# Fewer blocks turned through DRAM, and a turned load moved down its queue, in a forward-and-backward adaLN block on one core

## The chip, the core and the metric

The kernel runs on one core of a Trainium2 chip, written in Bass and Tile. The core has a matrix engine (TensorE, in the profile PE for matmuls and PEld for weight loads), a vector engine (VectorE, DVE), a scalar engine (ScalarE, ACT), GpSimd (POOL) and SyncE (SP). In this kernel SP issues nearly all loads and POOL nearly all stores: each of the two issues its DMAs strictly in the order of its program, and a DMA that has to wait for data or for a free buffer holds back all that stand behind it on that engine. The metric is the device time of one execution, in microseconds, as the median of three timed runs; one further execution is profiled.

## The reference: what is computed

One block of a network with a spectral mixer and a channel MLP, both modulated by a conditioning vector, and its gradient. S = 2048 tokens, D = 1024 channels, F = 3584 hidden units, all in bf16:

```python
def _A_ref(x, w_r, w_i):                       # spectral mixer
    X = rfft2(x.astype(float32)) * (w_r + 1j * w_i)
    return irfft2(X, s=(S, D)).astype(bfloat16)
def _B_ref(x, w1, b1, w2, b2):                 # channel MLP
    return gelu(layernorm(x) @ w1 + b1) @ w2 + b2
mod = silu(c) @ w_mod                          # six rows: sa, ca, ga, sb, cb, gb
h = layernorm(x) * (1 + ca) + sa
x = x + ga * _A_ref(h, w_r, w_i)
h = layernorm(x) * (1 + cb) + sb
x = x + gb * _B_ref(h, w1, b1, w2, b2)
```

The kernel returns the forward output and the gradients for grad_out of x, w_r, w_i, w1, b1, w2, b2, c and w_mod.

## The kernel before

Tokens are worked on in four blocks of 512, hidden units in 28 pieces of 128 (`fc`), channels in eight chunks of 128. Matmuls contract over the 128 partitions, so each matrix is needed with its contracted axis on the partitions. Where DRAM holds it the other way round, a transposing DMA (DMA_TRANSPOSE in the profile, `dma_start_transpose` in the code) turns it on the way in. The profile cuts the digits off the names: `d_n` is `d_n3`, `d_gx` is `d_gx1`, `d_x` is `d_x1`.

The stages follow each other on TensorE:

1. **Modulation, and the ph product beside the forward mixer.** ph is the gradient that reaches the hidden layer: w2 times the incoming gradient, which has been multiplied by gb (`gBoT`). `ph_part` (L803) computes for one `fc` and the four token blocks 32 matmuls into `pp`, and stores the result to `d_ph`. Its weights come from `wt`, a ring of two slots. Each slot holds a turned tile of 256 hidden units of w2, two `fc`; `load_w2t` (L339) loads tile `fg` on SP into slot `fg % 2`. Fourteen tiles pass through the ring. For the last four `fc` only two of the four token blocks are computed here and the other two a little later. Beside these products VectorE and ScalarE finish the mixer: `consume_fwd` (L849) adds, normalises and modulates one token block after the other and stores the normalised rows to `d_n3` on SP (L863).
2. **The MLP forward.** `z_block` (L916) loads a token block of `d_n3` turned (`n3Ta` for the first block, `n3Tb` for the next, L919), multiplies with w1 (`pz`, L931), applies the gelu and its derivative, and stores the hidden activations `d_hh` and their gradients `d_gz` by POOL. The seven w1 tiles are loaded by `load_w1` (L877) beside the last tiles of w2: two, one, and four of them.
3. **Back through w1.** For each token block `b`, `pg_pass` (L1088) multiplies gz with w1 turned, and VectorE and ScalarE go back through the two layer norms, with the block's rows `n3u`, `n2u` and `got` loaded on SP. The result is stored to `d_gx1` by POOL (L1312). In the same loop `turn` (L1250) prepares later stages: it loads a piece of `d_hh` or `d_gz` turned into one of two buffers `hb` (SP, L1253) and stores it in its new orientation to `d_hhT` or `d_gzT` (POOL, L1255). Ten `fc` of hh (10 to 19) are turned in the blocks b = 1 and 2, four pieces of gz in the block b = 3. At the end of the loop the last of the four `gB` tiles (the incoming gradient times gb) is computed by VectorE; two are loaded from `d_gB` (L1321).
4. **gw2 products and the backward mixer.** The gradient of w2: for each `fc`, `gw2_product` runs two groups of 16 matmuls of a turned hh block with the four `gB` tiles (L1221). The first two `fc` have their hh in `fbuf`; the others are loaded by `hh_load` within `pieces` (L1397) some products ahead: plainly from `d_hhT` for `fc` 10 to 19, and as a transposing DMA from `d_hh` for the others (tiles `hht`, `hhsA`, `otl`). Between the products stand the matmuls of the backward mixer.
5. **gw1 products.** The gradient of w1, in seven groups of 512 hidden units (L1440). Each group needs two tiles `gzh` of 1 MB, which `gw1_load` fetches: for the first group plainly from `d_gzT`, for the others by a transposing DMA from `d_gz`.

The order on each engine is written out by the program, with a scheduler that places instructions by priority; `tc.issue_after(x)` and `behind(y, x)` keep an instruction behind another one in the order. TensorE, VectorE and ScalarE have the same instructions in the same order in both kernels; only the queues of SP and POOL differ.

Of the kernel before, what the change touches and what calls it, by code (L numbers as in the profile page):

```python
# [11 lines left out]
BF16 = mybir.dt.bfloat16  # L12
# [5 lines left out]
P = 128  # L18
# [3 lines left out]
NT = S // P  # L22
# [9 lines left out]
BW = S // NB  # L32
# [3 lines left out]
def kernel(  # L36
# [24 lines left out]
    nc = tc.nc  # L61
# [5 lines left out]
    dram = ctx.enter_context(tc.tile_pool(name="dram", bufs=1, space=bass.MemoryType.DRAM))  # L67
# [40 lines left out]
    d_n3 = dram.tile([S, D], BF16, name="d_n3")  # L108
# [6 lines left out]
    d_SF = dram.tile([P, 4, 4, 512], BF16, name="d_SF")  # L115
    d_SI = dram.tile([P, 2, 4, 256], BF16, name="d_SI")
    d_E = dram.tile([P, 2, 8, 256], BF16, name="d_E")
    d_hhT = dram.tile([10, P, NT * P], BF16, name="d_hhT")
    d_gzT = dram.tile([4, P, NT * P], BF16, name="d_gzT")
    d_gmod = dram.tile([6 * D], BF16, name="d_gmod")  # L120
    d_ph_v = d_ph.rearrange("(fc p) s -> p fc s", p=P)
    d_hh_v = d_hh.rearrange("(fc p) s -> p fc s", p=P)
# [212 lines left out]
    go_f = tok_flat(grad_out)  # L335

    w2t_in = [None]

    def load_w2t(fg):  # L339
        w2t_in[0] = nc.sync.dma_start_transpose(out=wt[:, fg % 2], in_=B_w2[fg * 256:(fg + 1) * 256, :])  # L340

    x4s = [reg.tile([P, 4, D], BF16, name=f"x4_{i}", tag=f"uv{i}") for i in range(4)]
    fbuf = reg.tile([P, 4, 4, D], BF16, name="fbuf", tag="fr")
# [171 lines left out]
    def behind(ins, later):  # L515
        tc.add_manual_dep(ins.ins, later.ins.name, mybir.DependencyInfo(mybir.DependencyClass.NoSync, mybir.DependencyReason.DATA),
                          reason="order")
# [348 lines left out]
                  act_copy, act_copy, act_copy, consume_fwd, "fr")  # L866

    n3_sqrt, n3_norm = sqrt_in[0], norm_in[0]
    w1s = []
    w1_v = B_w1.rearrange("(c p) f -> p c f", p=P)  # L870

    def load_w1(n):
        for _ in range(n):
            g = len(w1s)
            wtile = reg.tile([P, NDC, BW], BF16, name=f"w1_{g}", tag=W1T[g])
            with tc.issue_after(w2t_in[0].ins):
                nc.sync.dma_start(out=wtile[:], in_=w1_v[:, :, g * BW:(g + 1) * BW])  # L877
            w1s.append(wtile)

    PH_KEEP = NFC - 4  # L880
# [35 lines left out]
    def z_block(b, g0, g1):  # L916
        n3T = n3Ts[b % 2]
        if g0 == 0:
            nc.sync.dma_start_transpose(out=n3T[:], in_=d_n3[b * BW:(b + 1) * BW, :])  # L919
        for g in range(g0, g1):  # L920
            n = b * 7 + g
            zb, av, bv, sg, ph = gts[n % 2]
# [3 lines left out]
            for k in range(4):  # L926
                fc = g * 4 + k
# [28 lines left out]
            for k in range(4 if b >= 2 else 0):  # L956
                fc = g * 4 + k
# [103 lines left out]
    def load_gz(b, g):  # L1061
        n = b * 7 + g
        gzs[b, g] = gzr[n % 8 // 2][:, n % 2]
        gz_in[0] = nc.sync.dma_start(out=gzs[b, g], in_=d_gz_v[:, g * 4:(g + 1) * 4, b * BW:(b + 1) * BW])
# [4 lines left out]
    for g in range(7):  # L1069
        wtile = reg.tile([P, 4, D], BF16, name=f"w1T_{g}", tag=W1T[g])  # L1070
        for k in range(4):
            fc = g * 4 + k
# [127 lines left out]
    def hh_in_frame(fc):  # L1200
        hh_in[0] = nc.sync.dma_start_transpose(out=hh_f[:, fc], in_=d_hh[fc * P:(fc + 1) * P, :])
# [9 lines left out]
    def sums3_ga(b, p4):  # L1211
        halves_sum(acc3[1], p4, b == 0, b == 3)
# [37 lines left out]
    def turn(dst, src, mm):  # L1250
        hb = reg.tile([P, mm, NT * P // mm], BF16, name="hb", tag=("gm", "sb")[turned[0] % 2])
        turned[0] += 1
        nc.sync.dma_start_transpose(out=hb[:], in_=src)  # L1253
        with tc.issue_after(gx_in[0].ins) if gx_in[0] else ExitStack():
            nc.gpsimd.dma_start(out=dst, in_=hb[:].rearrange("p a b -> p (a b)"))  # L1255

    for b in range(NB):
# [9 lines left out]
        if b > 0:  # L1267
            for g in range(7):
                load_gz(b, g)
            with tc.issue_after(gz_in[0].ins):  # L1270
                for k in range(5 if b < 3 else 0):
                    fc = 5 + 5 * b + k
                    turn(d_hhT[fc - 10], d_hh[fc * P:(fc + 1) * P, :], NT)
                for k in range(0 if b < 3 else 4):
                    turn(d_gzT[k], d_gz[0:512, k * 512:(k + 1) * 512], 4)
            if b == 2:
                hh_in_frame(0)
                hh_in_frame(1)
            for h in range(2):
                for _ in pg_pass(b, h, lambda k: ps_f):  # L1280
                    pass
            with tc.issue_after(last_pg[0].ins):
                sums3_ga(b - 1, au)
                if b == 2:
                    gb1_rows()
# [94 lines left out]
    w1g = {}  # L1380

    def gw1_load(fg):
        for k in range(2):
            if fg == 0:
                ins = nc.sync.dma_start(out=w1g["gz"][k][:].rearrange("p (j a) b -> p j (a b)", j=2),
                                        in_=d_gzT[2 * k:2 * k + 2].rearrange("j p n -> p j n"))
                continue
            ins = nc.sync.dma_start_transpose(out=w1g["gz"][2 * (fg % 2) + k][:],
                                              in_=d_gz[fg * 512:(fg + 1) * 512, k * 1024:(k + 1) * 1024])
        return ins  # L1390
# [5 lines left out]

    def pieces():  # L1397
        def hh_load(fc):
            if 10 <= fc < 20:
                hh_in[0] = nc.sync.dma_start(out=hh_s[hh_o[fc]].rearrange("p a b -> p (a b)"), in_=d_hhT[fc - 10])  # L1400
            else:
                hh_in[0] = nc.sync.dma_start_transpose(out=hh_s[hh_o[fc]], in_=d_hh[fc * P:(fc + 1) * P, :])
# [143 lines left out]
```

## Time and profile before

| | |
|---|---|
| timed runs | 1427.33, 1438.67 and 1431.37 us, median 1431.37 |
| profiled execution | 1444.82 us |
| its span | 1443.0 us, mean granted TensorE clock 0.985 |
| DVE, ACT, POOL busy | 1071.9, 744.5, 371.4 us |
| SP's DMA queue (q1) | 319558 packets, 207.18 MB, 55.5% of the 16 DMA engines' span |
| POOL's DMA queue (q0) | 37920 packets, 128.00 MB, 25.4% |

The span is what the profiler recorded between the first and the last instruction; the profiled execution's own time has some two microseconds around it, and lies 13.45 us above the median. The granted clock is the share of its full speed at which TensorE ran. The page cuts the span into 40 slices and gives the busy share of each engine in tenths:

```profile
PE   5999999799999999999999999969999999999998
DMA  9963647979787776697999499994889987767994
```

TensorE is at 9 nearly everywhere; besides the first slice two slices stand out, a 7 (the eighth slice, about 253 to 289 us) and a 6 (the 27th, about 938 to 974 us).

### The profile page before, as it was taken

To read this page: it belongs to the slowest core of one execution; us is meant where nothing else is said; L and a number is where in the kernel's file an instruction comes from. 1 tells how busy PE (TensorE), PEld (TensorE's weight loads), DVE (VectorE), ACT (ScalarE), POOL (GpSimd) and SP (SyncE) were. 2 spreads that over 40 slices of the span, in tenths; PEclk is the share of its full clock that TensorE was granted. 3 is DMA by queue.
4 is the path that set the end of the run, shared out by engine and by line. 5 is a ranking of instruction groups with operands and counts; after the bars stand their busy time and mean duration, and the time that the engine had idled before them with its cause. 6 is when DMAs were issued, how large, how long until landed. Compare 5 with 4: busy or idle time off the path is not lost. (4 is left out here: it accounts for less than half of the span.)

```text
span 1443.0 us, 18578 instructions
## 1 busy us (share of the span) xinstructions
PE 1370.7 (95%) x6839; PEld 662.9 (46%) x6963; DVE 1071.9 (74%) x1503; ACT 744.5 (52%) x1063; POOL 371.4 (26%) x482
## 2 busy tenths in 40 slices
PE   5999999799999999999999999969999999999998
PEld 2445674344444444444444444324554555444443
DVE  5898889867698877886610898949678668998633
ACT  4775766547977765666306564314433435444211
POOL 5601622200212122212110011011356541322323
PEclk8999999989999999999999999989999999999999
DMA  9963647979787776697999499994889987767994
GB/s 333 298 215 103 170 131 242 238 211 342 244 249 261 232 246 235 202 277 234 292 283 228 117 302 300 226 268 145 228 258 289 267 203 223 209 168 190 279 240 147
DMA packets 357569, 336.37 MB, mean 233 GB/s; under 512 B 207690, under 2 KB 297312, under 8 KB 357350
## 3 DMA queue, kind: packets, MB, share of 16 engines
q1 hardware_dynamic: 319558, 207.18, 55.5%
q0 software_dynamic: 37920, 128.00, 25.4%
q8 instruction: 54, 0.88, 0.3%
q14 instruction: 37, 0.30, 0.1%
HBM read 168.35 MB, written 117.49 MB: 198 GB/s over the span
## 5 line engine op out<-in xcount | busy, mean ns | idle before, releaser
L806 PE MATMUL pp<-gBoT,wt 128*128 128x512 bf16 x874 | 197.2, 383 | 13.6 <-DMA wt<-in_B_w_dram 12.5
L1088 PE MATMUL pg<-w1T,gzr 128*128 128x512 bf16 x877 | 195.0, 379 | 3.7 <-ACT gn3b L1103 1.7
L1440 PE MATMUL gw1acc<-gzh,n3n 128*128 128x512 bf16 x877 | 194.1, 379 | 1.0
L806 PEld LDWEIGHTS <-wt 128*128 128x128 bf16 x896 | 87.9, 98 | 117.5 <-DMA wt<-in_B_w_dram 13.0
L1088 PEld LDWEIGHTS <-gzr 128*128 128x128 bf16 x896 | 86.5, 98 | 110.7 <-issue 8.2
L931 PEld LDWEIGHTS <-w 128*128 128x128 bf16 x896 | 87.2, 98 | 107.3 <-issue 2.7
L1440 PEld LDWEIGHTS <-n3n 128*128 128x128 bf16 x896 | 87.3, 98 | 105.1 <-issue 1.3
L931 PE MATMUL pz<-n3Ta,w 128*128 128x512 bf16 x439 | 98.2, 379 | 1.8 <-ACT gt L934 1.3
L931 PE MATMUL pz<-n3Tb,w 128*128 128x512 bf16 x436 | 98.0, 379 | 0.7 <-issue 0.2
L934 ACT ACTIVATE gt<-pz,b_col 128x512 bf16<-128x512 f32 x112 | 73.3, 683 | 37.4 <-PE pz L931 36.9
L988 PEld LDWEIGHTS <-hhA 128*128 128x128 bf16 x608 | 58.9, 98 | 71.9 <-issue 1.6
L1221 PE MATMUL gw2acc<-gB,hhsA 128*128 128x512 bf16 x406 | 91.2, 379 | 0.5
L1444 ACT CAST gwo<-gw1acc 128x512 bf16<-128x512 f32 x49 | 28.5, 582 | 111.6 <-PE gw1acc L1440 102.8
L194 DVE TENSOR_TENSOR gt<-gt,gt 128x2048 bf16<-128x2048 bf16 x56 | 68.5, 1224 | 20.6 <-ACT gt L947 19.4
L945 ACT ACTIVATE gt<-gt 128x2048 bf16<-128x2048 bf16 x28 | 53.5, 1910 | 55.9 <-DVE gt L194 55.9
L194 DVE TENSOR_TENSOR ct<-ct 128x2048 bf16<-128x2048 bf16 x68 | 80.8, 1218 | 0.9
L1228 ACT CAST gwo<-gw2acc 128x512 bf16<-128x512 f32 x46 | 26.7, 582 | 100.9 <-PE gw2acc L1221 83.2
L1221 PEld LDWEIGHTS <-hhsA 128*128 128x128 bf16 x416 | 40.7, 98 | 47.9
L941 ACT ACTIVATE gt<-gt 128x2048 bf16<-128x2048 bf16 x28 | 53.5, 1910 | 1.8 <-DVE w2sA L194 1.1
L1445 POOL DMA_DIRECT2D out_dram<-gwo x56 | 30.7, 550 | 89.8 <-ACT gwo L1444 58.7
L947 ACT ACTIVATE gt<-gt 128x2048 bf16<-128x2048 bf16 x28 | 53.4, 1908 | 0.4
L812 ACT CAST pho<-pp 128x512 bf16<-128x512 f32 x59 | 33.6, 582 | 34.1 <-PE pp L806 32.8
(346 smaller groups left out, 2540.6 us busy)
## 6 DMA issues: line engine op xcount, KB each, us to landing
gzr<-d_gz SPq DMA_DIRECT2D x28, 512.0 KB
wblk<-in_w_mod_dram SPq DMA_DIRECT2D x12, 1024.0 KB
out_dram<-otl POOLq DMA_DIRECT2D x48, 256.0 KB, 4.2
out_dram<-gwo POOLq DMA_DIRECT2D x96, 128.0 KB, 4.4
d_ph<-pho POOLq DMA_DIRECT2D x21, 512.0 KB, 6.3
d_hh<-hhA POOLq DMA_DIRECT2D x19, 512.0 KB, 5.4
w<-in_B_w_dram SPq DMA_DIRECT2D x7, 1024.0 KB
hhC<-d_ph SPq DMA_DIRECT2D x14, 512.0 KB
```

The costliest lines, as they stand in the source:

```text
L194: return nc.vector.tensor_tensor(out=out, in0=a, in1=b, op=op)
L806: last_pe[0] = nc.tensor.matmul(pp[:], lhsT=wt[:, fg % 2, cch, k * P:(k + 1) * P], rhs=gBoT[j][:, cch, :], start=(cch == 0), stop=(cch == ...
L812: nc.any.tensor_copy(out=ov, in_=pv)
L931: last_pe[0] = nc.tensor.matmul(pz[:], lhsT=w1s[g][:, cch, k * P:(k + 1) * P], rhs=n3T[:, cch, :], start=(cch == 0), stop=(cch == NDC - 1))
L934: z_in = nc.scalar.activation(out=zb[:, k, :], in_=pz[:], func=ACT.Identity, bias=b1_col[:, fc:fc + 1], scale=1.0)
L941: nc.scalar.activation(out=av, in_=zb, func=ACT.Square)
L945: nc.scalar.activation(out=sg, in_=bv, func=ACT.Sigmoid, scale=2.0 * GK)
L947: nc.scalar.activation(out=bv, in_=bv, func=ACT.Sigmoid, scale=-2.0 * GK)
L988: last_pe[0] = nc.tensor.matmul(pbs[i][:], lhsT=hh[:, k, i * P:(i + 1) * P], rhs=wp[:, k, :], start=False, stop=(g == 6 and k == 3))
L1088: last_pg[0] = nc.tensor.matmul(pgs[i][:], lhsT=gzs[b, g][:, k, i * P:(i + 1) * P], rhs=w1Ts[g][:, k, h * KH:(h + 1) * KH], start=(g == 0 ...
L1221: nc.tensor.matmul(acc[:], lhsT=hh_of(fc)[:, t, :], rhs=gBs[t // 4][:, t % 4, h * KH:(h + 1) * KH], start=(t == 0), stop=(t == NT - 1))
L1440: nc.tensor.matmul(acc[:], lhsT=n3ns[t // 4][:, t % 4, cch * P:(cch + 1) * P], rhs=gz2[t // 8][:, t % 8, :], start=(t == 0), stop=(t == NT ...
```

## The change

There are three edits.

- **The first turned load of `d_n3` is moved.** The load of `n3Ta` stood on SP right behind the store of the first block of rows and ahead of the w2 tiles 10 and 11. Now it is issued behind w2 tile 11, and the first two w1 tiles are kept behind it. Between the two w1 tiles now stands the store of the second block of rows, where before both w1 tiles stood ahead of it. The new order on SP is: w2 tiles 10 and 11, `n3Ta`, w1 tile 0, second store of rows, w1 tile 1, w2 tile 12, w1 tile 2, w2 tile 13.
- **Nine blocks of hh are turned instead of ten.** `fc` 19 is no longer turned through DRAM; its later load in the gw2 stage becomes a transposing DMA from `d_hh`.
- **Two pieces of gz are turned instead of four.** The first `gzh` tile of the first gw1 group is still loaded plainly from `d_gzT`; the second becomes a transposing DMA of 1 MB from `d_gz`.

So three SP transposes into `hb` and three POOL stores out of it go away in stage 3, and two plain loads become transposing ones later.

```diff
-    d_hhT = dram.tile([10, P, NT * P], BF16, name="d_hhT")
-    d_gzT = dram.tile([4, P, NT * P], BF16, name="d_gzT")
+    d_hhT = dram.tile([9, P, NT * P], BF16, name="d_hhT")
+    d_gzT = dram.tile([2, P, NT * P], BF16, name="d_gzT")
...
     w2t_in = [None]
+    w2ts = []
 
     def load_w2t(fg):
         w2t_in[0] = nc.sync.dma_start_transpose(out=wt[:, fg % 2], in_=B_w2[fg * 256:(fg + 1) * 256, :])
+        w2ts.append(w2t_in[0])
...
-    w1s = []
+    w1s, w1_in = [], []
...
-                nc.sync.dma_start(out=wtile[:], in_=w1_v[:, :, g * BW:(g + 1) * BW])
+                w1_in.append(nc.sync.dma_start(out=wtile[:], in_=w1_v[:, :, g * BW:(g + 1) * BW]))
...
         if g0 == 0:
-            nc.sync.dma_start_transpose(out=n3T[:], in_=d_n3[b * BW:(b + 1) * BW, :])
+            with tc.issue_after(w2ts[11].ins) if b == 0 else ExitStack():
+                n3_in = nc.sync.dma_start_transpose(out=n3T[:], in_=d_n3[b * BW:(b + 1) * BW, :])
+            if b == 0:
+                for ins in w1_in[:2]:
+                    behind(ins, n3_in)
...
-                for k in range(5 if b < 3 else 0):
-                    fc = 5 + 5 * b + k
+                for fc in ((), range(10, 15), range(15, 19), ())[b]:
                     turn(d_hhT[fc - 10], d_hh[fc * P:(fc + 1) * P, :], NT)
-                for k in range(0 if b < 3 else 4):
+                for k in range(0 if b < 3 else 2):
                     turn(d_gzT[k], d_gz[0:512, k * 512:(k + 1) * 512], 4)
...
-            if fg == 0:
-                ins = nc.sync.dma_start(out=w1g["gz"][k][:].rearrange("p (j a) b -> p j (a b)", j=2),
-                                        in_=d_gzT[2 * k:2 * k + 2].rearrange("j p n -> p j n"))
+            if fg == 0 and k == 0:
+                nc.sync.dma_start(out=w1g["gz"][k][:].rearrange("p (j a) b -> p j (a b)", j=2),
+                                  in_=d_gzT.rearrange("j p n -> p j n"))
                 continue
...
-            if 10 <= fc < 20:
+            if 10 <= fc < 19:
                 hh_in[0] = nc.sync.dma_start(out=hh_s[hh_o[fc]].rearrange("p a b -> p (a b)"), in_=d_hhT[fc - 10])
```

## The prediction

> **What bounds the kernel now.** I read the page's head and groups first, then TensorE's waits, then the timeline of TensorE around the two places that the change touches, and last the queues that feed them. The page:
>
> ```profile
> span 1443.0 us, 18578 instructions
> PE 1370.7 (95%) x6839; PEld 662.9 (46%) x6963; DVE 1071.9 (74%) x1503; ACT 744.5 (52%) x1063; POOL 371.4 (26%) x482
> ...
> L806 PE MATMUL pp<-gBoT,wt 128*128 128x512 bf16 x874 | 197.2, 383 | 13.6 <-DMA wt<-in_B_w_dram 12.5
> ...
> L1221 PE MATMUL gw2acc<-gB,hhsA 128*128 128x512 bf16 x406 | 91.2, 379 | 0.5
> ```
>
> TensorE sets the time: it is idle for 1443.0 - 1370.7 = 72.3 us, and an edit that leaves its instructions alone can win at most these and what a low clock costs. TensorE's waits (what it waited for, total us, count, longest) say where the idle time is:
>
> ```profile
> PE pp L806 <- DMA wt<-in_B_w_dram: 12.5, 1, 12.5
> PE gw2acc L1221 <- DMA gB<-d_gB: 9.1, 2, 6.7
> PE gw2acc L1221 <- DVE gB L194: 2.6, 1, 2.6
> ```
>
> One wait for a turned w2 tile, and a cluster of waits at the first gw2 products. The timeline (start, length, instruction, in brackets the idle time ahead of it and its releaser) gives their sizes:
>
> ```profile
> 219.77 58.65 PE L806 MATMUL pp<-gBoT,wt 128*128 128x512 bf16 x266
> ...
> 290.95 44.15 PE L806 MATMUL pp<-gBoT,wt 128*128 128x512 bf16 x188 [12.53 <-DMA wt<-in_B_w_dram]
> 334.94 7.07 PE L931 MATMUL pz<-n3Ta,w 128*128 128x512 bf16 x32
> 341.85 13.98 PE L806 MATMUL pp<-gBoT,wt 128*128 128x512 bf16 x62
> ...
> 952.89 0.61 PE L217 MATMUL acc3b<-au,ones_bf 128*32 128x512 bf16 x8
> ...
> 970.68 13.07 PE L1221 MATMUL gw2acc<-gB,fbuf 128*128 128x512 bf16 x51 [2.59 <-DVE gB L194]
> 983.59 7.07 PE L1221 MATMUL gw2acc<-gB,hht 128*128 128x512 bf16 x32
> ```
>
> Thirty-two matmuls of one group take 341.85 - 334.94 = 6.91 us (0.216 each). One fc of the ph product is 32, so 6.91 us. **Stall A**: from 219.77 + 58.65 = 278.42 to 334.94 are 56.52 us; by the code they hold fc 20 to 23 whole and fc 24 to 27 half, 6 x 6.91 = 41.46 us. Lost: 15.1 us, 12.53 of it the wait, the rest the slow clock behind it (the windows' columns: us, busy of PE, PEld, DVE, ACT, POOL, the granted clock, DMA share, GB/s):
>
> ```profile
> 291.00:295.00 4.00, 4.00 (x10) 1.45 (x11) 0.41 (x1) 0.00 (x0) 0.00 (x0) 0.50 1.03 277
> ```
>
> **Stall B**: from 952.89 + 0.61 = 953.50 to 983.59 are 30.09 us for the 64 matmuls of one gw2 block (13.82 us). Lost: 16.3 us. A and B together are 31.4 us.
>
> **The change at stall A.** The SP queue there:
>
> ```profile
> 259.01 0.40 SPq L863 DMA_DIRECT2D d_n<-ct  x1
> 264.00 7.79 SPq L919 DMA_TRANSPOSE n3Ta<-d_n  x1
> 271.90 18.79 SPq L340 DMA_TRANSPOSE wt<-in_B_w_dram  x2
> ...
> 300.05 0.38 SPq L863 DMA_DIRECT2D d_n<-ct  x1
> 307.51 1.87 SPq L340 DMA_TRANSPOSE wt<-in_B_w_dram  x1
> ```
>
> SP issues in order. The load of n3Ta stands right behind the store of the rows that it reads, waits on SP until that has landed (264.00) and then holds SP for 7.79 us. The two w2 tiles behind it (numbers 10 and 11, read by fc 20 to 23) go out from 271.90; tile 10 ends the wait at 290.95. Its slot was free two fc earlier, at 278.42 - 13.82 = 264.6. After the change tiles 10 and 11 go ahead: tile 10 at 264.6, with 13.8 us to land, tile 11 at 278.4 when its slot comes free, with 13.8 us as well. n3Ta follows at about 280 and is read only at about 323 (334.94 less the gain), so its later issue costs nothing; if that cover went, its 7.79 us would stand ahead of the first pz product. The two w1 tiles follow n3Ta, the store of the second block of rows stands between them, then tile 12 (slot free at 292.2, read from 306.1) and tile 13.
>
> Not all 15.1 us come back, because VectorE's work of this stage is tied to the same products:
>
> ```profile
> 294.59 0.69 DVE L812 CAST pho<-pp 128x512 bf16<-128x512 f32 x1 [10.80 <-PE pp L806]
> ...
> 306.39 2.28 DVE L194 TENSOR_TENSOR ct<-ct,rows 128x4096 bf16<-128x4096 bf16 x1
> 308.59 1.22 DVE L194 TENSOR_TENSOR ct<-ct 128x2048 bf16<-128x2048 bf16 x1
> ```
>
> VectorE waited 10.80 us, not 15, at 294.59; what follows on it (306.39 on) moves some 11.7 us earlier (10.80 and part of the slow clock), and the products then wait for its evictions. The ring is also fuller: n3Ta and a w1 tile now stand ahead of the second store of rows, and VectorE's write at 308.59 needs that store to have read its tile; tile 12 follows them. I take 1.5 us for this. **A: 10 us**; its ends are 15 (nothing else late) and 2 (the wait moves on to tile 12 at 306.1; below).
>
> **The change at stall B.** The queues of SP and POOL, and VectorE:
>
> ```profile
> 919.04 10.95 SPq L1253 DMA_TRANSPOSE hb<-d_gz  x2
> ...
> 932.83 12.69 SPq L1253 DMA_TRANSPOSE hb<-d_gz  x2
> 945.57 1.25 SPq L1263 DMA_DIRECT2D n2u<-d_x  x1
> ...
> 947.57 0.97 SPq L1321 DMA_DIRECT2D gB<-d_gB  x2
> ```
> ```profile
> 950.21 0.53 POOL L1255 DMA_DIRECT2D d_gzT<-hb  x1 [5.23 <-DMA hb<-d_gz]
> 950.73 0.76 POOL L1312 DMA_DIRECT2D d_gx<-gn3a  x1
> ```
> ```profile
> 933.21 2.29 DVE L194 TENSOR_TENSOR gn3a<-gn3a,got 128x4096 bf16<-128x4096 bf16 x1
> ...
> 961.28 2.36 DVE L194 TENSOR_TENSOR gn3a<-pru 128x2048 bf16<-128x2048 bf16 x2 [19.18 <-DMA d_gx<-gn3a]
> 968.35 2.28 DVE L194 TENSOR_TENSOR gB<-got,rows 128x4096 bf16<-128x4096 bf16 x1
> ```
>
> Four gz pieces are turned here, each an SP transpose into one of two hb buffers and a POOL store out of it. Two things stand behind them. On SP, the loads of n2u, got and gB go out only from 945.57, so gB lands after TensorE wants it at 953.50. On POOL, the store of gn3a, whose data VectorE had finished at 933.21 + 2.29 = 935.5, goes out at 950.73, 15.2 us late, behind the store of the fourth piece. VectorE must not overwrite gn3a before that store has read it and waits 19.18 us; so the last gB block is computed from 968.35 to 970.63, and TensorE starts its full run at 970.68.
>
> The change takes pieces 3 and 4 away, 12.69 us of SP's queue and two POOL stores, and the turn of fc 19 ahead of them (the first gz piece takes its place, so the two that remain also end earlier). Then n2u goes out at about 932 to 933, where the third piece went out before, and the gB loads some 5 to 9 us later, once their buffers are free. Issued at 947.57, the first of them ended TensorE's wait at 953.50 + 6.7 = 960.2, 12.6 us later under a full ring; from 942 at the latest, under an emptier one, that is 950 to 954. The store of gn3a goes out at 935.5, takes at most the 961.28 - 950.73 = 10.55 us of before, less with the pieces gone; VectorE resumes at 942 to 946 instead of 961.28, and the last gB block ends some 17 us earlier (951 to 955) against 953.50. **B: 16.3 us** (ends 8 and 16.3; 8 if the gB loads or the store come only half as much earlier). The work behind it (VectorE's chain of the next block) moves by the same 17, so nothing there becomes late. The store and the transposes that are gone free bandwidth as well, which I count at nothing.
>
> **What it costs later.** fc 19's block is loaded by transpose from d_hh instead of plainly from its turned copy. The products that read hhsA mix blocks of both kinds of load and are idle for 0.5 us in all (the group above), so the prefetch covers either kind: 0 (0 to 1). The second half of the first gz tile of the gw1 stage (1 MB) becomes a transpose too:
>
> ```profile
> 1225.48 3.76 SPq L1388 DMA_TRANSPOSE gzh<-d_gz  x1
> 1229.42 0.46 SPq L1369 DMA_DIRECT2D xt<-d_gx  x1
> ...
> 1231.23 20.67 PE L1440 MATMUL gw1acc<-gzh,n3n 128*128 128x512 bf16 x93
> 1265.84 3.57 PE L740 MATMUL po<-gm,V 128*128 128x256 bf16 x28 [1.62 <-DVE eb L745]
> ...
> 1236.21 2.29 DVE L194 TENSOR_TENSOR ct<-ct,xt 128x4096 bf16<-128x4096 bf16 x1 [1.63 <-DMA xt<-d_gx]
> ```
>
> A transpose of this size holds SP 3.76 us where the plain load takes half of a pair; it goes out at about 1221.4, lands at about 1228 to 1230 and is read at about 1232.7, eight products into the group at 1231.23. But xt, for which VectorE already waits 1.63 us, comes some 2 us later, and TensorE waits for VectorE at 1265.84. **-2 us** (0 to -5). The Trainium skill ("DMA: Bandwidth & Descriptors", section "Latency and other measured facts") gives a transposing DMA 261 GB/s where the source's middle dimension is not contiguous and 350 to 400 GB/s where it is; 1 MB is then 4.0 or 2.6 to 3.0 us, an estimate by that page, near the 3.76 us of the row, and by it this term would be the same or smaller.
>
> **Sum in the profiled execution**: 10 + 16.3 - 2 = 24.3 us, 1443.0 to 1418.7 in span and 1444.8 to 1420.5 in time. But that execution was 1444.82 - 1431.37 = 13.45 us above the median of the three. These two stalls are 31.4 of 72.3 us of TensorE's idle time, so I give them the same share, 43%, of the 13.45: 5.8 us of them are not in the usual run. 24.3 - 5.8 = 18.5, and 1431.4 - 18.5 = **1413 us**.
>
> **The rivals.**
> *The whole gain is there in the median too*: 24.3 us or somewhat more, 1431.4 - 25 = 1406. For it: the cause in both places is the order of a queue, which is the same in each execution. Against: a DMA-bound stall is the natural place for a slow execution to be slow.
> *The wait moves to tile 12*: the queue now has n3Ta (1 MB), two w1 tiles and a store between tiles 11 and 12, and DMA was at its full share in the window quoted. Then A wins 2 to 5, and the sum is 3.5 + 16.3 - 2 - 5.8 = 12: 1419. For it: tiles 10 and 11 held SP for 18.79 us under that full ring. Against it: a tile like it held SP for only 1.87 us at 307.51, and it has 14 us.
> *Stall B goes only by half*, since the gB loads wait for buffers that VectorE frees, or the store of gn3a is slow by itself: 10 + 8 - 2 - 5 = 11, 1420. With the whole 13.45 us in the two stalls it is 24.3 - 13.45 = 10.9, the same time.
> *Slower: turned loads starve beside POOL's stores.* The page's line on packets, and those of the two kinds of queue from 281 to 287 (count, mean us of one, share):
>
> ```profile
> DMA packets 357569, 336.37 MB, mean 233 GB/s; under 512 B 207690, under 2 KB 297312, under 8 KB 357350
> ...
> q0 software_dynamic: 608, 2.29, 93.5%
> q1 hardware_dynamic: 603, 0.15, 11.3%
> ```
>
> SP's queue gets one packet for each of POOL's, 603 to 608, though POOL's are longer, 2.29 us to 0.15; that is about 100 packets per us. Most of the kernel's packets are under 512 bytes; I take 256 for a turned load, an estimate, so that a w2 tile (512 KB) is 2,048 packets and n3Ta 4,096: 20 and 41 us under a POOL queue that stays full. Then tile 12, behind tile 11 and n3Ta, lands at about 280 + 20 + 41 + 19 = 360 instead of by 306, TensorE loses 54 us where it lost 15.1, and with B and the late cost the time is 1431.4 + 39 - 16.3 + 2 + 2 = 1458. It decides if tile 12 lands after about 306 + 15 + 14 = 335. Against it: a POOL queue that is full for those 60 to 80 us would store 277 GB/s x 60 us = 17 MB, and by the code this stage has not half of it to store. The Trainium skill ("DMA: Bandwidth & Descriptors", section "Queues, rings and completion order") says that each DMA engine takes turns between its queues packet by packet; the trace agrees with 608 to 603.
> *It does nothing that can be measured*: the stalls refill from other waits, 1431.
>
> **How the numbers follow.** What a measurement of this kernel can tell from no change is about 1%, 14.3 us: faster is below 1417.1, slower above 1445.7. The forecast (1409 to 1417) has 0.48, the whole gain 0.13, the wait at tile 12 0.13, half of B or a smaller usual stall 0.13, nothing 0.06, slower 0.07. Faster 0.48 + 0.13 = 0.61, within 1% 0.32, slower 0.07. The range leaves out the slower rival and the tail of the others: down to 1431.4 - 31.4 = 1400, both stalls gone whole; up to 1429, where A gives 2, B 8, the late cost 5 and the stalls of the usual run are 3 smaller.
>
> **What the next profile would show.** A right: no wait of over 3 us for wt at fc 20 and none at fc 24, and from the end of fc 19 to the first pz product about 46 us, not 56.5. B right: the d_gx store goes out within 2 us of VectorE's write, VectorE waits under 10 us for it, and from the last au product to the first product with hht pass about 14 us, not 30.1. The late cost right: xt goes out some 2 us later against the first gw1 product, and the po product waits 3 to 4 us for VectorE. Wrong would be a wait for wt at fc 24, one for w1 or n3Ta at the first pz product, gB still landing behind 953, or a wait for gzh in gw1.

## The result, and the profile after

The changed kernel takes **1418.43 us** (median of 6, 1415.02 to 1421.32) where the kernel before, run beside it, takes 1431.57 us (median of 6, 1427.33 to 1444.43). The ratio is 0.989, with a 95% interval of 0.9848 to 0.9932: 15.7 us faster by the ratio, between 9.7 and 21.8. Its profiled execution took 1419.22 us, with a span of 1417.4 us; against the span of 1443.0 us before that is 25.6 us. Forecast were 18.5 us in time (1413 us) and 24.3 us in the profiled execution. The time lies inside the range of 1400 to 1429 us, but above the 1409 to 1417 us that stood for the forecast itself, and beside the 1419 us of the rival in which the wait moves to tile 12. So the sum made in the profile came out within 1.3 us of the gain, the time within 3, and the two gains differ by 10 us: 25.6 in the profile, 15.7 in time. What is behind this gap is what the experiments are about. (The ratios of this document leave out a single execution: one of 1437.18 us, of the kernel with only the order of the queues changed, which lies over 1.5% above the fastest of that kernel.)

The page of the changed kernel, head and the line of the ph product (columns as before: busy us, mean ns, then the idle time ahead and its releaser):

```profile
span 1417.4 us, 18569 instructions
PE 1367.5 (96%) x6839; PEld 663.0 (47%) x6963; DVE 1071.1 (76%) x1503; ACT 745.6 (53%) x1063; POOL 377.1 (27%) x479
...
L808 PE MATMUL pp<-gBoT,wt 128*128 128x512 bf16 x874 | 196.3, 381 | 4.0 <-DMA wt<-in_B_w_dram 2.8
```

TensorE's idle time fell from 72.3 to 49.9 us (1417.4 - 1367.5); the ph product waits 4.0 us instead of 13.6. The timeline of TensorE shows both places (start, length, instruction, idle time ahead of it and releaser):

```profile
220.27 86.28 PE L808 MATMUL pp<-gBoT,wt 128*128 128x512 bf16 x392
309.33 15.68 PE L808 MATMUL pp<-gBoT,wt 128*128 128x512 bf16 x62 [2.77 <-DMA wt<-in_B_w_dram]
324.84 7.07 PE L937 MATMUL pz<-n3Ta,w 128*128 128x512 bf16 x32
...
944.03 0.61 PE L217 MATMUL acc3b<-au,ones_bf 128*32 128x512 bf16 x8
944.58 13.99 PE L1227 MATMUL gw2acc<-gB,fbuf 128*128 128x512 bf16 x62
958.40 7.07 PE L1227 MATMUL gw2acc<-gB,hht 128*128 128x512 bf16 x32
```

**Place A**, from the first of these ph products to the first pz product: 324.84 - 220.27 = 104.6 us, before 334.94 - 219.77 = 115.2 us. The wait for tile 10 is gone; a new one of 2.77 us stands at tile 12 (309.33). SP's queue there (tiles 10 and 11, n3Ta, tile 12):

```profile
265.15 16.62 SPq L341 DMA_TRANSPOSE wt<-in_B_w_dram  x2
281.87 4.38 SPq L922 DMA_TRANSPOSE n3Ta<-d_n  x1
...
292.77 8.78 SPq L341 DMA_TRANSPOSE wt<-in_B_w_dram  x1
```

Tile 12 goes out when its slot comes free, at 292.77, but holds SP for 8.78 us and ends TensorE's wait only at 309.33, 16.6 us later; it had 13.8. **Place B**, from the end of the last product with au (944.03 + 0.61 = 944.64) to the first with hht: 958.40 - 944.64 = 13.8 us, before 30.1 us. Not a wait is left there. The two differences, 10.6 and 16.3 us, make 26.9; between and behind the two places 1.3 us net are given back.

What moved at place B, on POOL, on VectorE and on SP:

```profile
927.18 0.76 POOL L1317 DMA_DIRECT2D d_gx<-gn3a  x1 [4.03 <-issue]
```
```profile
924.35 2.29 DVE L194 TENSOR_TENSOR gn3a<-gn3a,got 128x4096 bf16<-128x4096 bf16 x1
...
933.28 2.36 DVE L194 TENSOR_TENSOR gn3a<-pru 128x2048 bf16<-128x2048 bf16 x2
...
940.35 2.29 DVE L194 TENSOR_TENSOR gB<-got,rows 128x4096 bf16<-128x4096 bf16 x1
```
```profile
923.02 0.36 SPq L1269 DMA_DIRECT2D n2u<-d_x  x1
...
930.32 3.81 SPq L1326 DMA_DIRECT2D gB<-d_gB  x2
```

The store of gn3a goes out 0.5 us after VectorE has finished its data (924.35 + 2.29 = 926.64), where it stood 15.2 us behind before. VectorE goes on at 933.28 without a wait (19.18 us before), and the last gB block is ready at 942.64 (940.35 + 2.29), ahead of the product that wants it at 944.64. On SP the gB loads go out 14.3 us ahead of that moment (944.64 - 930.32), where it was 5.9 us before (953.50 - 947.57).

### The profile page after: what moved, and what is told of

It is laid out like the page before. It is cut to its first block, busy times and chain, and to the rows that moved or that the text cites. A ratio compares the mean times of both kernels' runs of the same rounds, so it can differ in the third digit from the quotient of the medians.

```text
span 1417.4 us, 18569 instructions
## 1 busy us (share of the span) xinstructions
PE 1367.5 (96%) x6839; PEld 663.0 (47%) x6963; DVE 1071.1 (76%) x1503; ACT 745.6 (53%) x1063; POOL 377.1 (27%) x479
## 5 line engine op out<-in xcount | busy, mean ns | idle before, releaser
L1449 ACT CAST gwo<-gw1acc 128x512 bf16<-128x512 f32 x49 | 28.5, 582 | 111.0 <-PE gw1acc L1445 103.2
```

## The experiments

The theory behind the forecast: both stalls come from the order of the DMA queues, both are in every execution, and in the usual run each is smaller than in the profile. The rival that the time of the changed kernel brings up: one of the two is there in full, and the other hardly at all. In all runs the numbers of place A and place B are taken from TensorE's timeline as above; a ratio is to the kernel before, run on the same chip in the same session.

### The move alone

The kernel before with the first edit; ten hh blocks and four gz pieces are turned.

```diff
+            with tc.issue_after(w2ts[11].ins) if b == 0 else ExitStack():
+                n3_in = nc.sync.dma_start_transpose(out=n3T[:], in_=d_n3[b * BW:(b + 1) * BW, :])
+            if b == 0:
+                for ins in w1_in[:2]:
+                    behind(ins, n3_in)
```

> The kernel before with the move of the first turned load alone; all ten hh blocks and four gz pieces are turned. In the profile: from the first ph product of fc 12 to the first pz product 104.6 us as in the changed kernel (115.2 before), with the wait of some 2.8 us for w2 tile 12 still there, and the 30 us from the last au product to the first hht product unchanged. In time, theory (the usual run of the kernel before has both stalls, each a part smaller than its profile): about 6 us faster, ratio 0.996. Rival 1 (stall A is in every run as it is in the profile, and B is the one that varies): 10 us, 0.993. Rival 2 (stall A is large only in the slow profiled execution): 0 to 2 us, 0.999 to 1.

Measured: median 1431.35 us of 12 against 1434.79 us of 17, ratio 0.9983 (0.9964 to 1.0002), 2.4 us faster, between 5.2 faster and 0.3 slower. Its place A takes 103.2 us, as in the changed kernel, with a wait of 3.1 us for tile 12; place B takes 29.3 us. The profile did as forecast and the time did not: the theory's 6 us lies just outside the interval, and what came is rival 2.

### The turns alone

The kernel before with the second and third edits; n3Ta where it was.

```diff
+                for fc in ((), range(10, 15), range(15, 19), ())[b]:
                     turn(d_hhT[fc - 10], d_hh[fc * P:(fc + 1) * P, :], NT)
+                for k in range(0 if b < 3 else 2):
                     turn(d_gzT[k], d_gz[0:512, k * 512:(k + 1) * 512], 4)
...
+            if fg == 0 and k == 0:
...
+            if 10 <= fc < 19:
```

> The kernel before with nine hh blocks and two gz pieces turned, the first turned load where it was. In the profile: from the last au product to the first hht product 14 us (30.1 before); stall A at fc 20 unchanged, another sample of its size; the wait of the po product for VectorE in the gw1 stage 2.8 us as in the changed kernel (1.6 before). In time, theory: 16.3 less 1 to 2 for the late cost and less the part that is not in the usual run: about 10 us faster, ratio 0.993. Rival 1 (B is the one that varies): 4 to 6 us, 0.997. Rival 2 (A is the one that varies): 15 us, 0.990.

Measured: 1418.15 us, ratio 0.9892 (0.9866 to 0.9919), 15.5 us faster: the whole of the changed kernel's gain, without the move, as rival 2 had it. Place B takes 13.8 us. At place A, with the old order, there was almost nothing to win:

```profile
220.42 58.65 PE L806 MATMUL pp<-gBoT,wt 128*128 128x512 bf16 x266
279.45 31.25 PE L806 MATMUL pp<-gBoT,wt 128*128 128x512 bf16 x141 [0.38 <-DMA wt<-in_B_w_dram]
...
323.28 7.07 PE L931 MATMUL pz<-n3Ta,w 128*128 128x512 bf16 x32
```

The order on SP is that of the kernel before, and the wait for tile 10 is 0.38 us instead of 12.53: 102.9 us for the stage, less than the 104.6 of the changed kernel.

### The kernel before again

> The kernel before once more, for a second profiled execution of the same program. Theory (the wait for w2 tile 10 in the first profile was a chance of that execution, stall B is in every one): 102 to 106 us from the first ph product of fc 12 to the first pz product instead of 115.2, with a wait for wt under 3 us, and 29 to 30 us from the last au product to the first hht product. Rival (both stalls are the kernel's own): 110 to 116 us and 30 us.

Measured: 1434.02 us, and TensorE's timeline of the same program:

```profile
219.78 91.60 PE L806 MATMUL pp<-gBoT,wt 128*128 128x512 bf16 x415
312.86 8.79 PE L806 MATMUL pp<-gBoT,wt 128*128 128x512 bf16 x39 [1.48 <-DVE phr L812]
321.49 7.07 PE L931 MATMUL pz<-n3Ta,w 128*128 128x512 bf16 x32
...
951.46 1.89 PE L1221 MATMUL gw2acc<-gB,fbuf 128*128 128x512 bf16 x4 [7.29 <-DMA gB<-d_gB]
...
960.69 11.38 PE L1221 MATMUL gw2acc<-gB,fbuf 128*128 128x512 bf16 x51 [2.12 <-DVE gB L194]
971.91 7.07 PE L1221 MATMUL gw2acc<-gB,hht 128*128 128x512 bf16 x32
```

No wait for w2 at all, 101.7 us at place A (expected 102 to 106); at place B 27.7 us (expected 29 to 30), with the same three waits as in the first profile. Of these two executions of one program, stall A is in the first alone and stall B in both. How often stall A comes is shown further down.

### The order of the queues, with all pieces kept

```diff
-        nc.sync.dma_start_transpose(out=hb[:], in_=src)
+        late = turned[0] > 12
+        with tc.issue_after(gb_in.ins) if late else ExitStack():
+            nc.sync.dma_start_transpose(out=hb[:], in_=src)
-        with tc.issue_after(gx_in[0].ins) if gx_in[0] else ExitStack():
+        with tc.issue_after((gx_in[1] if late else gx_in[0]).ins) if gx_in[0] else ExitStack():
             nc.gpsimd.dma_start(out=dst, in_=hb[:].rearrange("p a b -> p (a b)"))
```

Twelve pieces (ten of hh, two of gz) keep their place, and `late` picks gz pieces 3 and 4.

> The kernel before with all ten hh blocks and four gz pieces, but the turned loads of gz pieces 3 and 4 behind the two gB loads on SP, and their stores behind the store of gn3a on POOL. Theory (stall B is the order of the two queues, not the amount of turning): from the last au product to the first hht product about 14 to 18 us instead of 30.1, with hht a little late since the two transposes now stand ahead of its loads; the same gain as the turns alone or 1 us more, since the late transposing load is not needed. Rival (the turned bytes themselves are the cost, through the DMA engines): the loss moves behind the gB loads, over 24 us stay, and the gain is under 4 us.

Measured: 1418.38 us (median of 6, 1414.34 to 1437.18), ratio 0.9885 (0.9857 to 0.9913), place B 956.35 - 942.59 = 13.8 us. TensorE, SP and POOL:

```profile
941.98 0.61 PE L217 MATMUL acc3b<-au,ones_bf 128*32 128x512 bf16 x8
956.35 7.07 PE L1221 MATMUL gw2acc<-gB,hht 128*128 128x512 bf16 x32
```
```profile
928.27 3.81 SPq L1323 DMA_DIRECT2D gB<-d_gB  x2
932.19 10.88 SPq L1255 DMA_TRANSPOSE hb<-d_gz  x2
```
```profile
925.29 0.76 POOL L1314 DMA_DIRECT2D d_gx<-gn3a  x1
943.72 0.58 POOL L1257 DMA_DIRECT2D d_gzT<-hb  x1 [11.67 <-DMA hb<-d_gz]
```

All ten blocks and four pieces are turned, and the gain is there in full. So turning three pieces more costs nothing that shows; their place in the two queues does. The delay that I expected at the first hht product did not come; a later one waits 2.0 us for its hht. The one execution of 1437.18 us was not profiled, and its cause is open.

### One hh block less, two gz pieces less, and one store earlier

Three parts of place B by themselves. The first two are the lines of the diff above taken singly: those on `fc` in the one, those on `k` in the other. The third keeps everything and puts only the store of gn3a ahead of the stores of pieces 3 and 4, on POOL:

```diff
-        with tc.issue_after(gx_in[0].ins) if gx_in[0] else ExitStack():
+        with tc.issue_after((gx_in[1] or gx_in[0]).ins) if turned[0] > 12 else tc.issue_after(gx_in[0].ins) if gx_in[0] else ExitStack():
             nc.gpsimd.dma_start(out=dst, in_=hb[:].rearrange("p a b -> p (a b)"))
```

> The kernel before with fc 19 of hh no longer turned; four gz pieces are turned and the first turned load is where it was. Theory (stall B is the place of the gn3a store and the gB loads in their queues): every gz piece moves up by one turn of about 6 us, the gn3a store goes out at about 944 instead of 950.7 (counted as in the profile before), the loss between the last au product and the first hht product falls from 16 to about 10 us: 6 us faster, 0.996. Rival (with two gz pieces less, fc 19 is not needed, and without that it does nothing): 0 to 2 us. In stage A, which is untouched, a further sample of the wait for w2 tile 10: theory (that wait was a chance of one execution) under 2 us and 102 to 105 us for the stage; rival (it is there in most executions) 110 us or more.

> The kernel before with two gz pieces turned instead of four; all ten hh blocks are turned. Theory: the gn3a store stands behind two pieces only and goes out when its data are there, 14 to 15 us between the last au product and the first hht product instead of 30, nearly all of the gain of the turns together: 14 to 16 us, 0.990. Rival (the gain goes by the amount of turning, two of three transposes and stores): 10 us, 0.993, and some 20 us between the two products. Stage A as in the run with nine hh blocks: under 2 us of wait for tile 10, if its wait was a chance.

> The kernel before with one order changed, on POOL alone: the store of gn3a stands ahead of the stores of gz pieces 3 and 4 instead of behind them. Theory (both queues hold the first gw2 products back, gB's loads on SP until about 964 and the last gB block behind the store until 970.7): the store goes out some 15 us earlier and the wait for VectorE's gB block goes, but the waits for the loaded gB tiles of 6 and 2 us stay: 24 to 28 us between the two products instead of 30, 2 to 6 us faster, 0.997. Rival 1 (the store is the whole cause): 14 to 16 us between the products and 15 us faster. Rival 2 (the store of gn3a matters to nobody): no change. Stage A as above.

Measured, beside the others; "lead" is the time from the issue of the gn3a store to the end of the last product with au:

| kernel | lead of the store, us | place B, us | ratio |
|---|---|---|---|
| before, two executions | 2.8 and 3.4 | 30.1 and 27.7 | 1 |
| the move alone | 3.8 | 29.3 | 0.9983 (0.9964 to 1.0002) |
| nine hh blocks | 9.4 | 23.8 | 0.9974 (0.9940 to 1.0008) |
| store first | 17.5 | 19.6 | 0.9947 (0.9910 to 0.9984) |
| two gz pieces | 17.5 | 13.8 | 0.9895 (0.9843 to 0.9948) |
| changed kernel | 17.5 | 13.8 | 0.9890 (0.9848 to 0.9932) |

One hh block less brings the store forward by some 6 us and shortens place B by 4 to 6, as the theory said; in time, 3.7 us, it cannot be told from nothing. With the two gz pieces gone it adds nothing to their gain. The store alone does more than I expected, 8 to 10.5 us at place B and 7.6 us in time, and less than the whole. The side expectation of these three runs, a wait for tile 10 of under 2 us at place A, failed in all of them: 3.1, 5.6 and 11.4 us. With the store first TensorE was at place B held by this:

```profile
951.81 0.61 PE L217 MATMUL acc3b<-au,ones_bf 128*32 128x512 bf16 x8
956.32 1.86 PE L1221 MATMUL gw2acc<-gB,fbuf 128*128 128x512 bf16 x4 [3.89 <-ACT gn3b L1103]
958.61 0.59 PE L1221 MATMUL gw2acc<-gB,fbuf 128*128 128x512 bf16 x1 [0.43 <-DMA gB<-d_gB]
```
```profile
951.06 4.64 ACT L510 ACTIVATE n2u<-n2u,stats 128x1024 bf16<-128x1024 bf16 x4 [20.28 <-DMA n2u<-d_x]
955.60 0.57 ACT L1103 ACTIVATE gn3b<-pg 128x512 bf16<-128x512 f32 x1
```

The last wait (for VectorE's gB block) is gone, and what remains lies at the start. The first wait, 3.89 us, is put down to an eviction by ScalarE, and the rows bear that out: `pg` and `gw2acc` take their buffers from the same pool in the code, and the first product starts at 956.32, 0.15 us after ScalarE has emptied the first of four `pg` (955.60 + 0.57). ScalarE comes to it so late because it normalises n2u first, for which it waited 20.28 us; and n2u stands on SP behind the gz pieces 3 and 4. In the kernel before, the same wait of ScalarE for n2u is there (20.65 us in the first profile), hidden by gB's load, which ended TensorE's wait 2.6 us after the first `pg` was empty (960.19 against 957.05 + 0.57). So SP's queue holds the first gw2 products in two ways, by gB and by n2u. Both queues count: by place B, POOL's store makes up 8 to 10.5 of the 14 to 16 us, by time about half (7.6 of 15.1 us with two gz pieces). No run changed SP's order alone.

### n3Ta at three other places

The changed kernel with n3Ta between tiles 10 and 11, behind tile 12, or behind tile 13 (the last). The edits, in this order:

```diff
+            with tc.issue_after(w2ts[10].ins) if b == 0 else ExitStack():
...
                 for ins in w1_in[:2]:
                     behind(ins, n3_in)
+                behind(w2ts[11], n3_in)
```
```diff
+            with tc.issue_after(w2ts[12].ins) if b == 0 else ExitStack():
...
-            if b == 0:
-                for ins in w1_in[:2]:
-                    behind(ins, n3_in)
```

```diff
-            with tc.issue_after(w2ts[11].ins) if b == 0 else ExitStack():
+            with tc.issue_after(w2ts[13].ins) if b == 0 else ExitStack():
                 n3_in = nc.sync.dma_start_transpose(out=n3T[:], in_=d_n3[b * BW:(b + 1) * BW, :])
             if b == 0:
-                for ins in w1_in[:2]:
+                for ins in w1_in[3:]:
                     behind(ins, n3_in)
```

Behind tile 12 and behind tile 13 the first two w1 tiles move too: they go out in n3Ta's old place, behind tile 11.

> The changed kernel with the load of n3Ta one w2 tile later still, behind tile 12, and w1 tiles no longer kept behind it. Theory (what is left of stall A is the ring crowded by n3Ta ahead of tile 12): the wait of 2.8 us for tile 12 goes, from the first ph product of fc 12 to the first pz product 101 to 103 us instead of 104.6, some 2 to 3 us faster than the changed kernel. Rival 1 (the w1 tiles crowd the ring just as well): 104 to 105 us, no difference. Rival 2 (n3Ta is now late at the first pz product): a wait for n3Ta of up to 8 us there, slower than the changed kernel.

> The changed kernel with n3Ta between w2 tiles 10 and 11, where SP waits anyway for tile 11's slot. Theory (tile 10 had no slack behind n3Ta, tile 12 has none behind n3Ta and the w1 tiles; between 10 and 11 n3Ta delays neither): no wait for wt over 1 us, 101 to 103 us from the first ph product of fc 12 to the first pz product (104.6 in the changed kernel), 1 to 3 us faster than the changed kernel. Rival (the DMA engines are full from 264 to 320 and a wait stays wherever n3Ta stands): 2 to 6 us of wait at tile 11 or 12, no difference or slower than the changed kernel.

> The changed kernel with n3Ta behind the last w2 tile and ahead of the fourth w1 tile. Theory: no wait for any w2 tile, but n3Ta goes out only at about 312, for a product at about 321.5: a wait of 0 to 6 us for n3Ta at the first pz product, 102 to 108 us for the stage, equal to or slower than the changed kernel. Rival (full engines, as above): the wait is over 6 us.

Beside the last two ran the changed kernel and the turns alone, once more:

> The changed kernel once more beside the three others. Theory: a wait of some 2.8 us for tile 12, 104 to 105 us for the stage, and times within some 8 us of each other; against the turns alone within 0.2%, with less spread. Rival (the move is worth its 10 us in most executions): 0.5% faster than the turns alone.

> The turns alone once more, beside the changed kernel. Theory (the wait for tile 10 in the old order goes with the DMA speed of the execution, 0 to 12 us): 102 to 115 us for the stage, the median within 0.2% of the changed kernel's and the slowest execution slower than its slowest. Rival as for the changed kernel: 0.5% slower than it.

Place A in every profiled execution of the study, by the place of n3Ta:

| n3Ta | place A, us (one number an execution) | wait for a w2 tile, us |
|---|---|---|
| ahead of tile 10 (as before) | 115.2, 101.7, 102.9, 105.7, 108.9, 113.2, 102.1, 112.6 | 12.5, 0, 0.4, 3.1, 5.6, 11.4, 0, 10.2, at tile 10 |
| behind tile 10 | 121.1 | 16.4, at tile 11 |
| behind tile 11 (the change) | 104.6, 103.2, 106.3 | 2.8, 3.1, 3.6, at tile 12 |
| behind tile 12 | 107.7 | 5.7, at tile 13 |
| behind tile 13 | 100.5 | none |

The means of the first and the third row are 107.8 and 104.7 us: by these few executions the move is worth about 3 us on average, not 10, and in three of the eight executions of the old order it would be worth nothing or less. The times do not show even that: the changed kernel takes 1419.21 us (1414.57 to 1421.6) with a ratio of 0.9893 (0.9858 to 0.9927), the turns alone 1417.09 us (1415.9 to 1427.38) with 0.9886 (0.9851 to 0.9921). The two cannot be told apart. The slowest of these six of the turns alone was the profiled one, with a wait of 10.2 us for tile 10; the six before them (1414.67 to 1422.09) have no such outlier.

My theory for n3Ta between tiles 10 and 11 fell. It was the worst place: ratio 0.995 (0.992 to 0.9981), 8.6 us slower than the changed kernel by the medians, and SP shows why:

```profile
264.91 4.05 SPq L341 DMA_TRANSPOSE wt<-in_B_w_dram  x1
269.07 16.19 SPq L922 DMA_TRANSPOSE n3Ta<-d_n  x1
285.36 16.90 SPq L341 DMA_TRANSPOSE wt<-in_B_w_dram  x1
```

n3Ta alone held SP for 16.19 us. Behind tile 12 the wait moved to the next w2 tile and grew to 5.7 us (ratio 0.9912, 0.9885 to 0.994). Behind the last tile nothing waits:

```profile
219.82 91.46 PE L808 MATMUL pp<-gBoT,wt 128*128 128x512 bf16 x415
311.68 8.79 PE L808 MATMUL pp<-gBoT,wt 128*128 128x512 bf16 x39 [0.40 <-DVE phr L814]
320.31 7.07 PE L937 MATMUL pz<-n3Ta,w 128*128 128x512 bf16 x32
```
```profile
308.07 4.40 SPq L922 DMA_TRANSPOSE n3Ta<-d_n  x1
```

n3Ta goes out at 308.07, 12.2 us ahead of its first product at 320.31, and there is no wait for it; I had expected 0 to 6 us. This version has the lowest median of all: 1415.37 us (of 4, 1414.58 to 1416.58), ratio 0.9873 (0.9832 to 0.9915), 18.2 us faster than before by the ratio and 3.8 us faster than the changed kernel beside it by the medians. All four lie below all 17 of the kernel before; with the changed kernel the ranges overlap. The profile speaks for a real step (100.5 against 103.2 to 106.3 us, no wait against 2.8 to 3.6), but it is one execution, so the step beyond the changed kernel is not shown.

### Why the wait for tile 10 comes and goes

All executions of the old order have the same instructions in the same order up to this place. Four of the eight ran on one chip, with waits of 0, 3.1, 5.6 and 11.4 us, so it is not the chip alone. The windows from 264 to 280 us, when n3Ta and tile 10 load beside POOL's stores, differ (columns: us, busy of PE, PEld, DVE, ACT, POOL, granted clock, DMA share, GB/s). The turns alone, second execution, wait 10.2 us:

```profile
264.00:280.00 16.00, 14.85 (x69) 6.57 (x67) 16.00 (x17) 8.06 (x14) 6.52 (x7) 1.00 1.18 177
```

The order of the queues with all pieces kept, no wait:

```profile
264.00:280.00 16.00, 15.95 (x74) 7.24 (x74) 16.00 (x17) 7.63 (x14) 6.25 (x6) 1.00 1.08 313
```

The DMA engines are full in both, and move 177 GB/s in the one and 313 in the other. The queues' view of the same two windows (packets, MB, share of 16 engines), in the same order:

```profile
q1 hardware_dynamic: 5583, 1.42, 80.2%
q0 software_dynamic: 406, 1.41, 38.2%
```
```profile
q0 software_dynamic: 936, 3.44, 59.6%
q1 hardware_dynamic: 6208, 1.57, 48.5%
```

A packet of SP's queue, nearly all of them turned loads here (1.57 MB is n3Ta's 1 MB and tile 10's half), takes 80.2% x 256 / 5583 = 37 ns in the slow one and 48.5% x 256 / 6208 = 20 ns in the quick one (256 is 16 us on 16 engines). The other executions of the old order have 161, 244, 259, 263, 278, 311 GB/s in this window for waits of 12.5, 11.4, 3.1, 5.6, 0.4 and 0 us. The 244 shows that this window is not all of it, and neither is n3Ta's hold on SP: 7.8, 5.5 and 4.2 us in the three executions with over 10 us of wait, 4.7 to 5.3 in the other five.

What follows has its part. In the first profile tile 10 had not landed at 280, and from 280 to 288 POOL's queue fills the engines:

```profile
q0 software_dynamic: 800, 3.02, 92.2%
q1 hardware_dynamic: 792, 0.20, 11.1%
```

SP's queue gets one packet for each of POOL's here, 99 per us, and its packets are short again (11.1% x 128 / 792 = 18 ns); the second execution of the turns alone has 661 to 654. In these two a tile 10 that was not through by 280 got on at POOL's pace. The third long wait (store first) has 1205 to 509 there, so this is not the whole cause either. With n3Ta behind tile 10 it is worse still, from 280 to 296:

```profile
q1 hardware_dynamic: 1677, 0.43, 83.6%
```

That is 83.6% x 256 / 1677 = 128 ns a packet. With n3Ta out of the window, the five executions have 4.53 to 4.63 MB from 264 to 280, all alike. So what varies is how fast n3Ta and tile 10 get through beside POOL's stores and gathers from 264 to 290 us; the traces count packets by queue and do not tell n3Ta's from tile 10's. What makes the packets slow in one execution and not in the next is open: no run changed POOL's side.

## Why the prediction was right or wrong

- **Stall B, 16.3 us: right, in mechanism and size.** Place B went from 27.7 to 30.1 us to 13.8 in each kernel with the store of gn3a and the gB loads ahead. The prediction's ends were 8 and 16.3; its bound of 10.55 us for the store was far on the safe side, VectorE did not wait for it at all (store at 927.18, VectorE's next write at 933.28). Keeping the pieces and changing only the order shows the cause; and the store alone, that both queues have a part in it. One path was missing: n2u's load, which the prediction names beside gB's, held TensorE too, through ScalarE's evictions. It left with the same edit, so the size came out all the same.
- **Stall A, 10 us: right in the profile, wrong in the time, and this is the step that failed.** The profile gave 10.6. But the term (tile 10 gets 13.8 us to land, 15.1 us are lost without the move) was read from one execution, in which the DMA engines moved 161 GB/s; in the seven others of the old order the stage lost 1.6 to 13.1 us against the 100.1 (115.2 - 15.1) that its matmuls take. The move measured 2.4 us in time (-0.3 to 5.2), 3.1 by the mean of the traces, and nothing in time beside the turns. The prediction did see that an execution 13.45 us above the median has too much of something, and named a DMA-bound stall as the natural place; then it spread the excess over both stalls in proportion, 5.8 us. The larger part belongs to A: the two profiled executions of this program, 1444.82 and 1434.02 us, lie 10.8 us apart, place A 115.2 - 101.7 = 13.5 and place B 30.1 - 27.7 = 2.4, and the rest gives some 5 back. That the profile's 10.6 met the forecast of 10 is luck: against the second profile of before the changed kernel's place A is 2.9 us longer.
- **No wait at fc 24: wrong.** The wait for tile 12 is there in all three executions of the changed order, 2.8 to 3.6 us: the rival that the wait moves on to tile 12 was part of the outcome. The prediction had put 1.5 us there, for the fuller ring, and had set against that rival that a tile like it had held SP for only 1.87 us; tile 12 held it for 8.78 us.
- **The late cost, -2 us: about 0.** From the start of the first run of 93 gw1 products to the long run behind the po products, the first profile of before has 42.1 us (1231.23 to 1273.37) and the changed kernel 43.2 (1204.57 to 1247.81), which looks like a cost of 1.1 us. But kernels that keep the plain load have 42.2 (store first), 42.9 (before again) and 43.2 (the move alone). xt was to come 2 us later; it goes out 1.6 us ahead of the first of these products and went out 1.8 us ahead before, which fits that SP had stood still from 1221.74 to 1225.48 before, long enough for the added transpose. The po product waits 2.8 us for VectorE, not 3 to 4, and 1.6 to 2.6 in the kernels that keep the plain load. fc 19's transposed load, taken at 0, cost nothing that shows: 0.5 us of idle time in the hhsA group before and after.
- **The slower rival, starving turned loads: not seen in the changed order**, but it was at work in the old one. It had 100 packets per us under a full POOL queue as the limit, by the equal numbers from 281 to 287. These 6 us lie inside the wait for tile 10 (278.42 to 290.95): the row that the prediction read as a threat to the new order is a part of the cause of stall A in the old one. In the slow window ahead of it the numbers are not equal, 5583 to 406, and the packets of SP's queue are long. The Trainium skill's rule of taking turns packet by packet ("DMA: Bandwidth & Descriptors", section "Queues, rings and completion order") speaks of the order of packets, and 792 to 800 agree with it; these runs show that their length varies as well, from 18 to 128 ns. The rival's sum has one term of 2 us that the prediction does not explain; without it the time would be 1456.
- **The sum**: 15.5 (turns) + 2.4 (move) are 17.9 us by the two single runs against 15.7 measured together, within their intervals. Forecast were 18.5. With the 5.8 us of discount shared out as 2.8 to A and 3.0 to B, that was 10 - 2.8 = 7.2 for the move, which measured 2.4, and 16.3 - 3.0 - 2 = 11.3 for the turns with their late cost, which measured 15.5: two errors of opposite sign, some 5 and 4 us, so that the total came this near is luck in part.

## What to carry to other kernels

A stall in one profile is a sample. Where the wait is for a DMA that lands just when it is needed, and the profiled execution lies above the median, look for the excess in that stall first, and take a second profile of the same kernel before an edit is built on it. Both stalls of this case came from the order of a queue; the one whose store stood 15 us behind its data was there in three executions of three (27.7 to 30.1 us), the one that hung on the speed of a load came and went (0 to 12.5 us). A bulk load with slack did best behind all loads with none, here behind the last tile of the ring, and worst between them, by one profile of each.

## What the runs showed of the hardware

- The same turned load of 1 MB held SP for 4.2 to 7.8 us ahead of tile 10, 16.2 us behind it, 4.4 to 4.6 us behind tile 11, 10.8 us behind tile 12 and 4.4 us behind tile 13; packets of SP's queue, nearly all turned loads, took 18 to 128 ns in windows in which all DMA engines were busy. A full DMA share says nothing of the rate: 1.18 went with 177 GB/s and 1.08 with 313.
- A short wait can cost more than itself. In the changed kernel the 62 matmuls behind the 2.77 us wait took 15.68 us; in the run with the move alone the same 62 took, behind a wait of 3.07 us:

```profile
309.00 13.99 PE L808 MATMUL pp<-gBoT,wt 128*128 128x512 bf16 x62 [3.07 <-DMA wt<-in_B_w_dram]
```

  The shorter wait cost 1.7 us of slower matmuls and the longer one none. From 310 to 313 us the granted clock was 0.50 in the changed kernel and 1.00 in the run with the move alone:

```profile
310.00:313.00 3.00, 3.00 (x8) 1.03 (x7) 3.00 (x5) 2.02 (x2) 0.00 (x0) 0.50 1.25 224
```
```profile
310.00:313.00 3.00, 3.00 (x16) 1.37 (x14) 3.00 (x6) 2.83 (x4) 0.53 (x1) 1.00 1.22 296
```

  The Trainium skill ("TensorE: Matmul & The Clock Gate", "Part 1: The HAM clock gate") says that TensorE's clock halves after an idle window of about 3.4 us and that the windows run freely. That it matters where in the window a wait falls would fit these rows; but 2.77 us cannot fill such a window, and the clock was halved all the same, so here the measurement goes against the rule as it stands. No run tested it further.
